# Hardware loops of two, five, eight and nine matmuls in an attention decode kernel, and a float32 turn of rows into columns per four heads

## The chip, the cores and the metric

The kernel runs on one core of a Trainium2 chip. The metric is the device time of one execution in microseconds (us), lower is better. Engines: PE multiplies matrices (PEld is its loading of weights, PEq or PEldq its sequencer), DVE is the vector engine, ACT the scalar engine, POOL the GpSimd engine; SP issues DMA transfers from a queue of its own. Each engine works through its own list of instructions in order and waits on semaphores that others raise.

## What is computed

A decode step for one token of width 640: a modulated layer norm, attention with 32 heads over a cache of 16384 positions of 128 each, and a gated feed-forward part. Cut to what matters:

```python
mod = (silu(c) @ w_mod).reshape(1, 6, 1, 640)        # c: (1, 640), w_mod: (640, 3840)
sa, ca, ga, sb, cb, gb = mod[:, 0], ..., mod[:, 5]
h = layernorm(x) * (1 + ca) + sa
q = (h @ wq).reshape(1, 1, 32, 128)                  # wq: (640, 4096)
scores = q . k_cache * 128 ** -0.5                   # k_cache, v_cache: (1, 32, 16384, 128)
o = softmax(scores) @ v_cache
x = x + ga * (o.reshape(1, 1, 4096) @ wo)            # wo: (4096, 640)
h = layernorm(x) * (1 + cb) + sb
x = x + gb * ((silu(h @ w_gate) * (h @ w_up)) @ w_down)   # F = 1728
```

All inputs are bfloat16. The caches are 268 of the 290 MB that are read.

## The kernel before

Every instruction is put down as an operation with an engine, a position in time (`pos`) and the operations that it depends on. `emit` sorts each engine's operations by position, and each engine then runs them in that order. There is no other scheduler: where an operation stands in its engine's queue is its position.

Sizes: H = 32 heads, TT = 128 positions per partition, KC = 5 pieces of 128 of the width, GQ = 4. `TK(h)` is the nominal start of head h, 20 + 19.8 h; `TL` is that of the last head.

**Start.** SP issues w_mod, wq, the four pieces of K of head 0 and K of head 1. PE multiplies the first two of w_mod's six parts (`mod_mm_a`), then q for all heads in eight groups (L352), each copied by ACT to `qbc`. Behind them in PE's queue stands `mod_mm_b` at position 4.5: the other four parts, 4 x 5 columns of five 128x1 matmuls each (100), from `f_mod` (L330), all written out. ACT copies its result (`mod_b`, L369, position 4.6). The operation `onep_b` on DVE (L370) reads that copy; it stands at `TK(0) + 19.3`, ahead of all DVE work of head 1.

**One head.** DVE multiplies K by q (L433), folds the products three times (L435, L442), sums (L445) and takes the largest (L448). POOL takes the largest over partitions (`gm`, L451), ACT scales it (`nb`, L453) and exponentiates (L455); POOL sums (`L`, L458), ACT forms the reciprocal (`lnl`, `rl`, L460 and L462). Then PE makes the value product (L471): 32 matmuls of four columns of P with 512 columns of V, so that the four 128-wide diagonal blocks of a 4x512 result hold the sum. Two matmuls stand ahead of a hardware loop, two behind it, and the loop has seven turns of `PVB` = 4 (L476). ACT scales the result into `acc_sb` (L483, four partitions, float32), and `diag` (L490) turns the rows into a column of `OT_ps` with four float32 matmuls against `ident_f`, one head at a time. ACT copies it (`on`, L511), spreads it over `Z` (L514), and once for a group of heads one matmul (L518) and one copy (`as`, L520) put the group in the order in which wo's rows lie. The groups are 8, 8, 8 and 4 heads; heads 28 to 31 (from `HD` on) go without a group, straight into `On` (L523).

**Queues.** SP's queue has, for each head, K of head h + 1 at `TK(h) + 8.8` (waits for the sum of head h - 1, whose place it takes) and V of head h just behind it at `TK(h) + 8.9` (waits for the value product of head h - 2). ACT's queue has `acc` of head h at `TK(h) + 28.6`, which is ahead of `nb` and `exp` of head h + 1 at `TK(h+1) + 19.2` and `+ 19.4`. PE's queue at the end: value product of head 30, its `diag`, then wo for the groups (`f_wo`, L559, positions from `TL + 29.45`, written out: 28 rows of five matmuls), wo for heads 28 to 30 (`TL + 29.48`), the last head (L501, `TL + 29.5`), wo for head 31 (`TL + 29.8`), layer norm, gate, up, down.

**The last head** has V in three pieces (`VSPLIT`: 64, 32 and 32 of the 128 positions), and 128 written-out matmuls of 128x128 by one column, straight into the column of `OT_ps`.

**The end.** The transfers of the feed-forward weights take the place of K and wait for the last head's sum. Gate and up (L623) have 70 matmuls each, down (L641) 70 in five pieces.

Of the kernel before, what the change touches and what calls it, by code (L numbers as in the profile page):

```python
# [7 lines left out]
F32 = mybir.dt.float32  # L8
ALU = mybir.AluOpType
ACTF = mybir.ActivationFunctionType  # L10
# [26 lines left out]
class _Plan:  # L37
# [104 lines left out]
def build(nc, A_x, A_k, A_v, A_wq, A_wo, B_wg, B_wu, B_wd, c_in, w_mod, out):  # L142
    H, S, Dh = A_k.shape[1], A_k.shape[2], A_k.shape[3]
    D = A_x.shape[2]
    F = B_wg.shape[1]
    assert Dh == 128 and D % 128 == 0 and S % 128 == 0
    KC = D // 128
    TT = S // 128
# [2 lines left out]
    FCH = NF + (1 if FR else 0)  # L151
    NP2 = NF // 2
    GQ = 4
    PVB = 4

    GROUPS = [(0, 8), (8, 8), (16, 8), (24, 4)]
    HD = 28
# [10 lines left out]
    with es:  # L168
# [3 lines left out]
        def sb(name, shape, dtype):  # L172
            return es.enter_context(nc.sbuf_tensor(name, list(shape), dtype))
# [17 lines left out]
        wg_v = kflat[:, 0:KC * F].rearrange("p (k n) -> p k n", k=KC)  # L191
        wu_v = kflat[:, KC * F:2 * KC * F].rearrange("p (k n) -> p k n", k=KC)
        wd_v = kflat[:, 2 * KC * F:2 * KC * F + FCH * D].rearrange("p (k n) -> p k n", k=FCH)
        acc_sb = sb("acc_sb", [4, 2, 512], F32)
        ident_f = sb("ident_f", [4, 4], F32)
        qbc = sb("qbc", [128, H, 128], BF16)
        S_sb = sb("S_sb", [128, 2, TT], F32)
        P_sb = sb("P_sb", [128, 2, TT], BF16)
# [19 lines left out]
        rl = sb("rl", [128, H], F32)  # L218
# [106 lines left out]
        def f_mod(e, wv, m0, m1, cols):  # L325
            last = None
            for m in range(m0, m1):
                for k in range(KC):
                    for kd in range(KC):
                        last = e.matmul(mod_ps[:, m * KC + k:m * KC + k + 1],  # L330
                                        lhsT=wv[:, kd, cols(m * D, k)], rhs=silu_c[:, kd:kd + 1],
                                        start=(kd == 0), stop=(kd == KC - 1))
            return last
# [31 lines left out]
        o_q_all = list(o_q.values())  # L365


        o_mod_b = op(PE, 4.5, lambda e: f_mod(e, wm_v, 2, 6, lambda o, k: slice(o + 128 * k, o + 128 * (k + 1))), deps=[d_wm, o_h], name="mod_mm_b")
        o_modc = op(ACT, 4.6, lambda e: e.activation(out=modb[:], in_=mod_ps[:, 2 * KC:6 * KC], func=ACTF.Copy), deps=[o_mod_b], name="mod_b")  # L369
        o_onep_b = op(DVE, TK(0) + 19.3, lambda e: e.tensor_scalar_add(out=onep_b[:], in0=modb[:, 2 * KC:3 * KC], scalar1=1.0), deps=[o_modc], name="onep_b")  # L370
        ga, sb_, gb = modb[:, 0:KC], modb[:, KC:2 * KC], modb[:, 3 * KC:4 * KC]
# [32 lines left out]
        load_k(0)  # L404
        load_k(1)

        o_idf = op(ACT, 4.7, lambda e: e.activation(out=ident_f[:], in_=ident[0:4, 0:4], func=ACTF.Copy), deps=[o_ident], name="ident_f")
        o_msk, o_e8 = {}, {}
        for n in msk:
            o_msk[n] = op(DVE, TK(0) + 19.0, lambda e, n=n: e.tensor_reduce(  # L410
# [8 lines left out]
        for h in range(H):  # L419
# [46 lines left out]
            if h < H - 1:  # L466


                def f_pv(e, s2=s2):
                    def one(t, at, start=False, stop=False):  # L470
                        return e.matmul(acc_ps[s2][0:4, :], lhsT=P_sb[:, s2, bass.ds(t, 4)],  # L471
                                        rhs=vbig[:, bass.ds(at, 512)], start=start, stop=stop)
                    v0 = s2 * TT * 128
                    one(0, v0, start=True)
                    one(4, v0 + 512)
                    with e.Fori(0, (TT - 16) // (4 * PVB)) as i:  # L476
                        for u in range(PVB):
                            one(i * (4 * PVB) + (8 + 4 * u), i * (512 * PVB) + (v0 + 1024 + 512 * u))
                    one(TT - 8, v0 + 128 * (TT - 8))
                    return one(TT - 4, v0 + 128 * (TT - 4), stop=True)  # L480
                o_pvlast[h] = op(PE, base + 28.0, f_pv, deps=[o_exp[h], d_v[h][0], o_acc[h - 2] if h >= 2 else o_qev[H // GQ - 1],
                                                              o_qev[H // GQ - 2]], name="pv%d" % h)
                o_acc[h] = op(ACT, base + 28.6, lambda e, h=h, s2=s2: e.activation(  # L483
                    out=acc_sb[:, s2], in_=acc_ps[s2][0:4, :], func=ACTF.Copy, scale=rl[0:4, h:h + 1]),
                    deps=[o_pvlast[h], o_rl, o_diag[h - 2] if h >= 2 else None], name="acc%d" % h)

                def f_diag(e, h=h, s2=s2):
                    last = None
                    for i in range(4):
                        last = e.matmul(OT_ps[:, h:h + 1], lhsT=acc_sb[:, s2, 128 * i:128 * (i + 1)], rhs=ident_f[:, i:i + 1],  # L490
                                        start=(i == 0), stop=(i == 3))
                    return last
                o_diag[h] = op(PE, base + 28.8, f_diag, deps=[o_acc[h], o_idf], name="diag%d" % h)
                done, sc = o_diag[h], 1.0
            else:

                for c in range(len(VSPLIT) - 1):
                    def f_pv(e, h=h, s2=s2, c=c):
                        last = None
                        for t in range(VSPLIT[c], VSPLIT[c + 1]):  # L500
                            last = e.matmul(OT_ps[:, h:h + 1], lhsT=vring[:, s2, t, :], rhs=P_sb[:, s2, t:t + 1],  # L501
                                            start=(t == 0), stop=(t == TT - 1))
                        return last
                    prev = op(PE, base + 29.5 + 0.05 * c, f_pv, deps=[o_exp[h], d_v[h][c], prev], name="pv%d_%d" % (h, c))
                o_pvlast[h] = prev
                done, sc = prev, rl[:, h:h + 1]
            if h < HD:
                g = [i for i, (h0, n) in enumerate(GROUPS) if h0 <= h < h0 + n][0]
                h0, n = GROUPS[g]
                jw = 128 // n  # L510
                o_on[h] = op(ACT, base + 29.0, lambda e, h=h, sc=sc: e.activation(  # L511
                    out=on_f[:, h:h + 1], in_=OT_ps[:, h:h + 1], func=ACTF.Copy, scale=sc),
                    deps=[done, o_rl], name="on%d" % h)
                o_z[h] = op(ACT, base + 29.2, lambda e, h=h, g=g, n=n, o=(h - h0) * jw, jw=jw: e.activation(  # L514
                    out=Z[:, g, o:o + jw], in_=msk[n][:], func=ACTF.Copy, scale=on_f[:, h:h + 1]),
                    deps=[o_on[h], o_msk[n]], name="z%d" % h)
                if h == h0 + n - 1:
                    o_am = op(PE, base + 29.4, lambda e, g=g, n=n: e.matmul(A_ps[:, 0:n], lhsT=Z[:, g], rhs=e8[n][:], start=True, stop=True),  # L518
                              deps=[o_z[i] for i in range(h0, h0 + n)] + [o_e8[n], o_as[g - 1] if g else None], name="am%d" % g)
                    o_as[g] = op(ACT, base + 29.6, lambda e, h0=h0, n=n: e.activation(out=A_sb[:, h0:h0 + n], in_=A_ps[:, 0:n], func=ACTF.Copy),  # L520
                                 deps=[o_am], name="as%d" % g)
            else:
                o_on[h] = op(ACT, base + 29.0 + (0.7 if h == H - 1 else 0.0), lambda e, h=h, sc=sc: e.activation(  # L523
                    out=On[:, h - HD:h - HD + 1], in_=OT_ps[:, h:h + 1], func=ACTF.Copy, scale=sc),
                    deps=[done, o_rl], name="on%d" % h)


        TO = TL + 9.0
# [2 lines left out]
        while a < len(GROUPS):  # L531
            b = a
            while b < len(GROUPS) and GROUPS[b][1] == GROUPS[a][1]:
# [6 lines left out]
            a = b  # L540
        d_wo1 = plan.dma(TO + 0.1, wo_v[:, HD:H, :], A_wo[HD * 128:H * 128, :].rearrange("(k p) n -> p k n", p=128),
                         "wo1", deps=[o_mod_b, o_mod], name="dma_wo_rows")
        wo_seq = [(k, g) for g, (h0, n) in enumerate(GROUPS) for k in range(h0, h0 + n)] + [(k, None) for k in range(HD, H)]
        o_wo = []
        for g in list(range(len(GROUPS))) + [None] * (H - HD):
            if g is not None:
                ks = [k for k, gg in wo_seq if gg == g]
                deps, pos = [o_as[g], d_wo[g]], TL + 29.45 + 0.005 * g
            else:
                k = HD + len(o_wo) - len(GROUPS)  # L550
                ks = [k]
                deps, pos = [o_on[k], d_wo1], TL + (29.48 + 0.001 * (k - HD) if k < H - 1 else 29.8)

            def f_wo(e, ks=ks):
                last = None
                for k in ks:
                    rhs = A_sb[:, k:k + 1] if k < HD else On[:, k - HD:k - HD + 1]
                    for cc in range(KC):
                        last = e.matmul(attn_ps[:, cc:cc + 1], lhsT=wo_v[:, k, 128 * cc:128 * (cc + 1)], rhs=rhs,  # L559
                                        start=(k == 0 and cc == 0), stop=(k == H - 1 and cc == KC - 1), skip_group_check=True)  # L560
                return last
            o_wo.append(op(PE, pos, f_wo, deps=deps, name="wo%d" % len(o_wo)))


        HX = H // 2
# [135 lines left out]
```

## Time and profile before

| | us |
|---|---|
| median of three runs | 686.17 (685.95 to 686.21) |
| the profiled execution | 685.94 |
| its span, first to last instruction | 684.2 |
| PE busy | 352.1 (51%) |
| DVE busy | 617.5 (90%) |
| ACT busy | 79.9 (12%) |
| POOL busy | 376.6 (55%) |

A row of a view's group or timeline has: when it starts, how long it takes (or the busy time of a group), the engine, the line of the kernel, the operation, what is written and what is read, the shape, the count, and in brackets the idle time just ahead and what ended it. The page's strips divide the span into 40 equal slices; a digit is the busy share of a slice in tenths. Matmuls are pipelined, so their durations overlap. Instructions that only PE's sequencer runs (register arithmetic, moves, branches) are not counted as busy; the view of a single source line lists them under PEldq, with the least, the median and the largest duration in ns.

Some groups that the change touches, before:

```profile
L490 PE MATMUL psb<-ident_f,acc_sb 4*128 4x1 f32 x248 | 32.5, 248 | 23.9 <-ACT acc_sb L483 23.9
L483 ACT ACTIVATE acc_sb<-psb,rl 4x512 f32<-4x512 f32 x31 | 21.0, 679 | 165.1 <-PE psb L471 165.1
L514 ACT ACTIVATE Z<-msk,on_f 128x16 bf16<-128x16 f32 (+1 forms) x28 | 8.7, 310 | 0.9
L511 ACT ACTIVATE on_f<-psb 128x1 f32<-128x1 f32 x28 | 4.8, 171 | 31.9 <-PE psb L490 30.7
```

### The profile page before, as it was taken

The numbers are of one execution on the slowest core, as the hardware profiler recorded it, in microseconds if no ns is written. First come the engines' busy times: TensorE is split into PE (matmuls) and PEld (weight loads), VectorE is DVE, ScalarE is ACT, GpSimd is POOL, SyncE is SP. The second block draws the span as 40 slices with busy tenths as digits, with TensorE's granted clock in tenths as the row PEclk, the third lists the DMA queues.
The fourth block names the chain that finished last, engine by engine and source line by source line (L and its number), as shares of the span: only waits on it lengthen the run. The fifth ranks groups of instructions, "written<-read, shape, count | busy, mean of one in ns | idle before, by whom it ended". The sixth has DMA issues, their size and how long they took to land.

```text
span 684.2 us, 6294 instructions
## 1 busy us (share of the span) xinstructions
PE 352.1 (51%) x1951; PEld 151.0 (22%) x1952; DVE 617.5 (90%) x226; ACT 79.9 (12%) x281; POOL 376.6 (55%) x71
## 2 busy tenths in 40 slices
PE   2335245565555444556544544656544446565554
PEld 1122022222212112222211212222121112221254
DVE  0299999999999999999999999999999999999911
ACT  1111011011101111011101111011011110110010
POOL 0004765655567765655567766655564656555600
PEclk9967666767777776776777776676677766766765
DMA  9999999999999999999999999999999999999996
GB/s 374 418 437 431 431 436 433 430 431 433 435 428 429 429 433 429 435 431 430 437 433 432 432 427 431 428 433 429 432 433 433 435 435 428 431 431 432 412 413 267
DMA packets 13689, 290.70 MB, mean 425 GB/s; under 512 B 1318, under 2 KB 2024, under 8 KB 4200
## 3 DMA queue, kind: packets, MB, share of 16 engines
q1 hardware_dynamic: 13668, 290.48, 99.2%
q8 instruction: 10, 0.16, 0.1%
q14 instruction: 7, 0.06, 0.0%
q10 hardware_dynamic: 4, 0.00, 0.0%
HBM read 290.48 MB, written 0.00 MB: 425 GB/s over the span
## 4 chain that ended last, share of the span: by engine, by line
DVE 79%; DMA 18%; SPq 2%; issue 1%; PE 0%; ACT 0%; DVEq 0%
DVE kring L433 35%; DVE kring L435 18%; DVE kring L442 14%; DMA kring<-in_A_k_cache_dram 12%; DVE S_sb L445 9%; DMA vbig<-in_A_wq_dram 4%; DMA kring<-in_B_w_down_dram 2%; SPq L71 2%; DVE pm L448 1%; PE psb L352 0%; PE psb L641 0%; ACT qbc L356 0%; DVE e L415 0%; DVE msk L410 0%; PE psb L649 0%
## 5 line engine op out<-in xcount | busy, mean ns | idle before, releaser
L471 PE MATMUL psb<-vbig,P_sb 128*4 128x512 bf16 (+1 forms) x992 | 285.4, 458 | 267.0 <-ACT P_sb L455 200.3
L451 POOL PARTITION_ALL_REDUCE gm<-pm x32 | 254.8, 7963 | 226.7 <-DVE pm L448 220.6
L433 DVE TENSOR_TENSOR kring<-kring,qbc 128x16384 bf16<-128x16384 bf16 (+1 forms) x35 | 278.4, 7954 | 14.0 <-ACT qbc L356 12.9
L471 PEld LDWEIGHTS psb<-vbig,P_sb 128*4 128x4 bf16 (+1 forms) x992 | 94.6, 97 | 444.7 <-ACT P_sb L455 243.5
L435 DVE TENSOR_TENSOR kring<-kring 128x8192 bf16<-128x8192 bf16 (+1 forms) x35 | 142.1, 4059 | 1.2
L458 POOL PARTITION_ALL_REDUCE Ls<-rs x32 | 120.8, 3774 | 29.9 <-ACT P_sb L455 29.9
L442 DVE TENSOR_TENSOR kring<-kring 128x4096 bf16<-128x4096 bf16 x64 | 112.5, 1758 | 2.2
L445 DVE TENSOR_REDUCE S_sb<-kring 128x128 f32<-128x2048 bf16 x32 | 73.2, 2286 | 1.1
L490 PE MATMUL psb<-ident_f,acc_sb 4*128 4x1 f32 x248 | 32.5, 248 | 23.9 <-ACT acc_sb L483 23.9
L483 ACT ACTIVATE acc_sb<-psb,rl 4x512 f32<-4x512 f32 x31 | 21.0, 679 | 165.1 <-PE psb L471 165.1
L490 PEld LDWEIGHTS psb<-ident_f,acc_sb 4*128 4x128 f32 x248 | 29.8, 186 | 39.6 <-ACT acc_sb L483 39.6
L453 ACT ACTIVATE nb<-gm 128x1 f32<-128x1 f32 x32 | 6.5, 202 | 213.2 <-POOL gm L451 213.2
L460 ACT ACTIVATE lnl<-Ls 128x1 f32<-128x1 f32 x32 | 6.5, 203 | 124.7 <-POOL Ls L458 124.7
L352 PE MATMUL psb<-vbig,h_col 128*128 128x512 bf16 x39 | 9.9, 421 | 10.6 <-DMA vbig<-in_A_wq_dram 10.6
L598 DVE TENSOR_TENSOR tt<-attn_bf,modb 128x5 f32<-128x5 bf16 x1 | 0.2, 166 | 15.3 <-ACT attn_bf L597 15.3
L455 ACT ACTIVATE P_sb<-S_sb,nb 128x128 bf16<-128x128 f32 x32 | 12.9, 402 | 1.2
L448 DVE TENSOR_REDUCE pm<-S_sb 128x1 f32<-128x128 f32 x32 | 9.2, 286 | 1.1
L514 ACT ACTIVATE Z<-msk,on_f 128x16 bf16<-128x16 f32 (+1 forms) x28 | 8.7, 310 | 0.9
L511 ACT ACTIVATE on_f<-psb 128x1 f32<-128x1 f32 x28 | 4.8, 171 | 31.9 <-PE psb L490 30.7
L352 PEld LDWEIGHTS psb<-vbig,h_col 128*128 128x128 bf16 x40 | 4.2, 108 | 15.9 <-DMA vbig<-in_A_wq_dram 10.3
L356 ACT ACTIVATE qbc<-psb 128x512 bf16<-128x512 f32 x8 | 4.8, 598 | 23.2 <-PE psb L352 23.2
L330 PE MATMUL psb<-silu_c,wreg 128*128 128x1 bf16 x150 | 4.8, 168 | 5.0 <-DMA wreg<-in_w_mod_dram 5.0
(74 smaller groups left out, 67.0 us busy)
## 6 DMA issues: line engine op xcount, KB each, us to landing
kring<-in_A_k_cache_dram SPq DMA_DIRECT2D x31, 4096.0 KB, 18.3
vbig<-in_A_v_cache_dram SPq DMA_DIRECT2D x31, 4096.0 KB, 27.5
vbig<-in_A_wq_dram SPq DMA_DIRECT2D x1, 5120.0 KB, 26.3
wreg<-in_w_mod_dram SPq DMA_DIRECT2D x1, 4800.0 KB, 14.4
kring<-in_A_k_cache_dram SPq DMA_DIRECT2D x4, 1024.0 KB, 31.3
wreg<-in_A_wo_dram SPq DMA_DIRECT2D x1, 3840.0 KB, 37.9
kring<-in_B_w_gate_dram SPq DMA_DIRECT2D x1, 2160.0 KB, 18.4
kring<-in_B_w_up_dram SPq DMA_DIRECT2D x1, 2160.0 KB, 23.8
```

Source lines behind the costliest of these rows:

```text
L71: return e.dma_start(out_ap, in_ap)
L352: last = e.matmul(q_ps[b][:, 0:n * 128], lhsT=h_col[:, k:k + 1].broadcast_to([128, 128]), rhs=wv[:, k, n0:n0 + n * 128], start=(k == 0), s ...
L433: o_m = op(DVE, base + 3.3 * c, lambda e, ksl=ksl, qb=qb: e.tensor_tensor(out=ksl, in0=ksl, in1=qb, op=ALU.mult), deps=[d_k[h][c], o_qbc[h ...
L435: fd.append(op(DVE, base + 3.3 * c + 2.2 + (6.6 if npc == 1 else 0.0), lambda e, ksl=ksl: e.tensor_tensor(out=ksl[:, :, 0:64], in0=ksl[:, ...
L442: prev = [op(DVE, base + 15.5 + 1.5 * i, lambda e, kslot=kslot, w=w: e.tensor_tensor(out=kslot[:, :, 0:w], in0=kslot[:, :, 0:w], in1=kslot ...
L445: o_red[h] = op(DVE, base + 18.2, lambda e, s2=s2, kslot=kslot, w=w: e.tensor_reduce(out=S_sb[:, s2], in_=kslot[:, :, 0:w], axis=AX.X, op= ...
L448: o_max = op(DVE, base + 18.5, lambda e, h=h, s2=s2: e.tensor_reduce(out=pm[:, h:h + 1], in_=S_sb[:, s2], axis=AX.X, op=ALU.max), deps=[o_ ...
L451: o_gm = op(POOL, base + 19.0, lambda e, h=h: e.partition_all_reduce(gm[:, h:h + 1], pm[:, h:h + 1], channels=128, reduce_op=bass.bass_isa ...
L458: o_L = op(POOL, base + 20.0, lambda e, h=h: e.partition_all_reduce(Ls[:, h:h + 1], rs[:, h:h + 1], channels=128, reduce_op=bass.bass_isa. ...
L471: return e.matmul(acc_ps[s2][0:4, :], lhsT=P_sb[:, s2, bass.ds(t, 4)], rhs=vbig[:, bass.ds(at, 512)], start=start, stop=stop)
L483: o_acc[h] = op(ACT, base + 28.6, lambda e, h=h, s2=s2: e.activation(out=acc_sb[:, s2], in_=acc_ps[s2][0:4, :], func=ACTF.Copy, scale=rl[0 ...
L490: last = e.matmul(OT_ps[:, h:h + 1], lhsT=acc_sb[:, s2, 128 * i:128 * (i + 1)], rhs=ident_f[:, i:i + 1], start=(i == 0), stop=(i == 3))
```

## The change

Five edits, four of them on PE.

1. **Value loop.** `PVB` is 2 instead of 4. One matmul stands ahead of the loop and one behind it, and the loop has 15 turns of two.
2. **Rows into columns per four heads.** `acc_sb` has 128 partitions. Head j of four writes partitions 32 j to 32 j + 3 in one of two halves. One `diag` for four heads (for three at the end) sums over all 128 partitions against `sel`, which picks one of the four rows for each head; `acc_sb` is set to zero once on DVE (`acc_zero`, position 2.3). The copies `on` take four columns at once; `Z` is still filled head by head.
3. **Second half of w_mod.** 19 turns of a loop of five matmuls, and the last column written out.
4. **wo for the groups.** One operation instead of four: five matmuls written out, then 27 turns of five. It waits for all four groups and all their transfers.
5. **The last head.** 63 of the first piece's 64 matmuls in seven turns of nine, the second piece's 32 in four turns of eight; the third piece stays written out.

```diff
-    PVB = 4
+    PVB = 2
...
-        acc_sb = sb("acc_sb", [4, 2, 512], F32)
-        ident_f = sb("ident_f", [4, 4], F32)
+        acc_sb = sb("acc_sb", [128, 2, 512], F32)
+        sel = sb("sel", [128, 4, 4], F32)
...
-        o_mod_b = op(PE, 4.5, lambda e: f_mod(e, wm_v, 2, 6, lambda o, k: slice(o + 128 * k, o + 128 * (k + 1))), deps=[d_wm, o_h], name="mod_mm_b")
+        def f_mod_b(e):
+            def column(i):
+                last = None
+                for kd in range(KC):
+                    last = e.matmul(mod_ps[:, bass.ds(i + 2 * KC, 1)], lhsT=wreg[:, bass.ds(i * 128 + (kd * 6 + 2) * D, 128)],
+                                    rhs=silu_c[:, kd:kd + 1], start=(kd == 0), stop=(kd == KC - 1))
+                return last
+            with e.Fori(0, 4 * KC - 1) as i:
+                column(i)
+            return column(4 * KC - 1)
+        o_mod_b = op(PE, 4.5, f_mod_b, deps=[d_wm, o_h], name="mod_mm_b")
...
+        o_az = op(DVE, 2.3, lambda e: e.memset(acc_sb[:], 0.0), deps=[o_cc, o_xc0, o_sc], name="acc_zero")
...
                     one(0, v0, start=True)
-                    one(4, v0 + 512)
-                    with e.Fori(0, (TT - 16) // (4 * PVB)) as i:
+                    with e.Fori(0, (TT - 8) // (4 * PVB)) as i:
                         for u in range(PVB):
-                            one(i * (4 * PVB) + (8 + 4 * u), i * (512 * PVB) + (v0 + 1024 + 512 * u))
-                    one(TT - 8, v0 + 128 * (TT - 8))
+                            one(i * (4 * PVB) + (4 + 4 * u), i * (512 * PVB) + (v0 + 512 + 512 * u))
                     return one(TT - 4, v0 + 128 * (TT - 4), stop=True)
...
+                if j == GQ - 1 or h == H - 2:
+                    def f_diag(e, h0=h - j, n=j + 1, gb_=gb_):
+                        last = None
+                        for i in range(4):
+                            last = e.matmul(OT_ps[:, h0:h0 + n], lhsT=acc_sb[:, gb_, 128 * i:128 * (i + 1)], rhs=sel[:, i, 0:n],
+                                            start=(i == 0), stop=(i == 3))
+                        return last
+                    o_diag[h] = op(PE, base + 28.8, f_diag, deps=o_acc[h - j:h + 1] + [o_sel], name="diag%d" % h)
...
                     def f_pv(e, h=h, s2=s2, c=c):
+                        def one(t):
+                            return e.matmul(OT_ps[:, h:h + 1], lhsT=vbig[:, bass.ds(t * 128 + s2 * TT * 128, 128)], rhs=P_sb[:, s2, bass.ds(t, 1)],
+                                            start=(isinstance(t, int) and t == 0), stop=(isinstance(t, int) and t == TT - 1))
+                        ta, tb = VSPLIT[c], VSPLIT[c + 1]
                         last = None
-                        for t in range(VSPLIT[c], VSPLIT[c + 1]):
-                            last = e.matmul(OT_ps[:, h:h + 1], lhsT=vring[:, s2, t, :], rhs=P_sb[:, s2, t:t + 1],
-                                            start=(t == 0), stop=(t == TT - 1))
+                        if c < len(VSPLIT) - 2:
+                            if c == 0:
+                                one(0)
+                                ta = 1
+                            n = max(n for n in range(1, 11) if (tb - ta) % n == 0)
+                            with e.Fori(0, (tb - ta) // n) as i:
+                                for u in range(n):
+                                    one(i * n + (ta + u))
+                            return None
+                        for t in range(ta, tb):
+                            last = one(t)
                         return last
...
+        def f_wo_cols(e):
+            for cc in range(KC):
+                e.matmul(attn_ps[:, cc:cc + 1], lhsT=wo_v[:, 0, 128 * cc:128 * (cc + 1)], rhs=A_sb[:, 0:1],
+                         start=(cc == 0), stop=False, skip_group_check=True)
+            with e.Fori(0, HD - 1) as i:
+                for cc in range(KC):
+                    e.matmul(attn_ps[:, cc:cc + 1], lhsT=wreg[:, bass.ds(i * D + (D + 128 * cc), 128)], rhs=A_sb[:, bass.ds(i + 1, 1)],
+                             start=False, stop=False, skip_group_check=True)
+            return None
+        o_wo.append(op(PE, TL + 29.45, f_wo_cols, deps=o_as + d_wo, name="wo_cols"))
```

`bass.ds(a, n)` is a slice of n elements from a, where a may be formed from the loop's counter; `e.Fori(0, n)` is a loop that the engine's own sequencer runs.

More of the change, by code (lines that the diff above doesn't have):

```diff
@@ L405, in build @@
         load_k(1)
-        o_idf = op(ACT, 4.7, lambda e: e.activation(out=ident_f[:], in_=ident[0:4, 0:4], func=ACTF.Copy), deps=[o_ident], name="ident_f")
+        o_sel = op(ACT, 4.7, lambda e: e.activation(
+            out=sel[:], in_=ident[:].rearrange("p (j c) -> p c j", j=4)[:, 0:4, :], func=ACTF.Copy), deps=[o_ident], name="sel")
+        o_az = op(DVE, 2.3, lambda e: e.memset(acc_sb[:], 0.0), deps=[o_cc, o_xc0, o_sc], name="acc_zero")
         o_msk, o_e8 = {}, {}
@@ L480, in f_pv @@
                     return one(TT - 4, v0 + 128 * (TT - 4), stop=True)
+                j, gb_ = h % GQ, (h // GQ) % 2
                 o_pvlast[h] = op(PE, base + 28.0, f_pv, deps=[o_exp[h], d_v[h][0], o_acc[h - 2] if h >= 2 else o_qev[H // GQ - 1],
                                                               o_qev[H // GQ - 2]], name="pv%d" % h)
-                o_acc[h] = op(ACT, base + 28.6, lambda e, h=h, s2=s2: e.activation(
-                    out=acc_sb[:, s2], in_=acc_ps[s2][0:4, :], func=ACTF.Copy, scale=rl[0:4, h:h + 1]),
-                    deps=[o_pvlast[h], o_rl, o_diag[h - 2] if h >= 2 else None], name="acc%d" % h)
@@ L487, in f_diag @@
[L487 to L494, printed above, removed]
+                o_acc[h] = op(ACT, base + 28.6, lambda e, h=h, s2=s2, j=j, gb_=gb_: e.activation(
+                    out=acc_sb[32 * j:32 * j + 4, gb_], in_=acc_ps[s2][0:4, :], func=ACTF.Copy, scale=rl[0:4, h:h + 1]),
+                    deps=[o_pvlast[h], o_rl, o_diag[h - 2 * GQ + GQ - 1 - j] if h >= 2 * GQ else o_az], name="acc%d" % h)
@@ L498, in f_pv @@
                     def f_pv(e, h=h, s2=s2, c=c):
+                        def one(t):
+                            return e.matmul(OT_ps[:, h:h + 1], lhsT=vbig[:, bass.ds(t * 128 + s2 * TT * 128, 128)], rhs=P_sb[:, s2, bass.ds(t, 1)],
+                                            start=(isinstance(t, int) and t == 0), stop=(isinstance(t, int) and t == TT - 1))
+                        ta, tb = VSPLIT[c], VSPLIT[c + 1]
                         last = None
-                        for t in range(VSPLIT[c], VSPLIT[c + 1]):
-                            last = e.matmul(OT_ps[:, h:h + 1], lhsT=vring[:, s2, t, :], rhs=P_sb[:, s2, t:t + 1],
-                                            start=(t == 0), stop=(t == TT - 1))
+                        if c < len(VSPLIT) - 2:
[9 more added lines that the diff above has]
+                            last = one(t)
                         return last
-                    prev = op(PE, base + 29.5 + 0.05 * c, f_pv, deps=[o_exp[h], d_v[h][c], prev], name="pv%d_%d" % (h, c))
+                    prev = op(PE, base + 29.5 + 0.05 * c, f_pv, deps=[o_exp[h], d_v[h][c]], name="pv%d_%d" % (h, c))
                 o_pvlast[h] = prev
-                done, sc = prev, rl[:, h:h + 1]
             if h < HD:
@@ L510, in build @@
                 jw = 128 // n
[L511 to L516, printed above, removed]
+                if j < GQ - 1:
+                    continue
+                o_on[h] = op(ACT, base + 29.0, lambda e, h=h: e.activation(
+                    out=on_f[:, h - GQ + 1:h + 1], in_=OT_ps[:, h - GQ + 1:h + 1], func=ACTF.Copy),
+                    deps=[o_diag[h]], name="on%d" % h)
+                for hh in range(h - GQ + 1, h + 1):
+                    o_z[hh] = op(ACT, base + 29.2, lambda e, h=hh, g=g, n=n, o=(hh - h0) * jw, jw=jw: e.activation(
+                        out=Z[:, g, o:o + jw], in_=msk[n][:], func=ACTF.Copy, scale=on_f[:, h:h + 1]),
+                        deps=[o_on[h], o_msk[n]], name="z%d" % hh)
                 if h == h0 + n - 1:
@@ L521, in build @@
                                  deps=[o_am], name="as%d" % g)
[L522 to L525, printed above, removed]
+            elif h == H - 2:
+                o_on[h] = op(ACT, base + 29.0, lambda e: e.activation(
+                    out=On[:, 0:H - 1 - HD], in_=OT_ps[:, HD:H - 1], func=ACTF.Copy), deps=[o_diag[h]], name="on%d" % h)
+                for hh in range(HD, h):
+                    o_on[hh] = o_on[h]
+            elif h == H - 1:
+                o_on[h] = op(ACT, base + 29.7, lambda e, h=h: e.activation(
+                    out=On[:, h - HD:h - HD + 1], in_=OT_ps[:, h:h + 1], func=ACTF.Copy, scale=rl[:, h:h + 1]),
+                    deps=[prev, o_rl], name="on%d" % h)
         TO = TL + 9.0
@@ L542, in build, with f_wo @@
                          "wo1", deps=[o_mod_b, o_mod], name="dma_wo_rows")
-        wo_seq = [(k, g) for g, (h0, n) in enumerate(GROUPS) for k in range(h0, h0 + n)] + [(k, None) for k in range(HD, H)]
         o_wo = []
[L545 to L554, printed above, removed]
-                last = None
[L556 to L560, printed above, removed]
+        def f_wo_cols(e):
[8 more added lines that the diff above has]
+        o_wo.append(op(PE, TL + 29.45, f_wo_cols, deps=o_as + d_wo, name="wo_cols"))
+        for k in range(HD, H):
+            def f_wo(e, k=k):
+                last = None
+                for cc in range(KC):
+                    last = e.matmul(attn_ps[:, cc:cc + 1], lhsT=wo_v[:, k, 128 * cc:128 * (cc + 1)], rhs=On[:, k - HD:k - HD + 1],
+                                    start=False, stop=(k == H - 1 and cc == KC - 1), skip_group_check=True)
                 return last
-            o_wo.append(op(PE, pos, f_wo, deps=deps, name="wo%d" % len(o_wo)))
+            o_wo.append(op(PE, TL + (29.48 + 0.001 * (k - HD) if k < H - 1 else 29.8), f_wo, deps=[o_on[k], d_wo1], name="wo%d" % k))
         HX = H // 2
```

## The prediction

> **What bounds the kernel now.** I read the page's strips first, then the timeline at both ends, then the instructions of the loop that already exists.
>
> ```profile
> span 684.2 us, 6294 instructions
> DMA  9999999999999999999999999999999999999996
> q8 instruction: 10, 0.16, 0.1%
> ```
>
> The transfers run full from the first slice to the last but one. The chain of waits gives DVE 79% of the span, and both are true. From 51.70 us on, DVE starts a head every 19.28 us, and the transfers deliver a head's K and V in 19.42 us (K landings 48.1, 67.5, 86.96). Until 492 us DVE is never idle between heads, and from 495 us it waits for K. Thirty periods from 51.70 end at 630.2 us, while the last head's first product starts at 632.06. So DVE has 1.9 us to spare in the whole run, and the transfers have none. The hand-over from PE to DVE in the first head is this:
>
> ```profile
> 37.82 2.64 PE L330 MATMUL psb<-silu_c,wreg 128*128 128x1 bf16 x100
> 40.50 0.19 ACT L369 ACTIVATE modb<-psb 128x20 f32<-128x20 f32 x1 [1.88 <-PE psb L330]
> 51.63 0.16 DVE L370 TENSOR_SCALAR onep_b<-modb 128x5 f32<-128x5 f32 x1
> 51.70 8.68 DVE L433 TENSOR_TENSOR kring<-kring,qbc 128x16384 bf16<-128x16384 bf16 x1
> ```
>
> The second half of the modulation product takes 2.64 us and is ready 11 us before DVE reads it, in the instruction just ahead of the second head. The end of the run on PE:
>
> ```profile
> 651.33 1.05 PE L490 MATMUL psb<-ident_f,acc_sb 4*128 4x1 f32 x8 [0.77 <-ACT acc_sb L483]
> 652.31 3.68 PE L559 MATMUL psb<-A_sb,wreg 128*128 128x1 bf16 x140
> 659.42 1.85 PE L501 MATMUL psb<-P_sb,vbig 128*128 128x1 bf16 x64 [1.69 <-DMA vbig<-in_A_v_cache_dram]
> 664.30 0.67 PE L501 MATMUL psb<-P_sb,vbig 128*128 128x1 bf16 x19 [1.47 <-DMA vbig<-in_A_v_cache_dram]
> 670.05 2.25 PE L623 MATMUL psb<-h_col,kring 128*128 128x1 bf16 x70 [1.04 <-DVE h_col L607]
> 675.37 2.25 PE L623 MATMUL psb<-h_col,kring 128*128 128x1 bf16 x70 [3.06 <-DMA kring<-in_B_w_up_dram]
> 679.48 0.69 PE L641 MATMUL psb<-gu_col,kring 128*128 128x1 bf16 x20 [0.57 <-DMA kring<-in_B_w_down_dram]
> ```
>
> PE works off wo and the last head between transfers and waits again for w_up and w_down. It is near the end without setting it. Written out, a 128x1 product costs it 26 ns (3.68 us / 140) to 29 ns (1.85 / 64).
>
> **What a loop costs on PE.** The view of one line's instructions also lists what PE's sequencer runs, for the value loop (L471, loop line L476):
>
> ```profile
> L471 PEldq FUSED_REGOPS  x868: 51/74/79, 58.2 to 649.3; - x174
> L476 PEldq FUSED_REGOPS  x217: 78/78/82, 58.1 to 648.7; - x109
> L476 PEldq ALU_OP  x217: 36/36/42, 58.8 to 649.4; - x109
> L476 PEldq COMPARE_BRANCH  x217: 76/213/353, 58.9 to 649.5; - x109
> ```
>
> That is 31 heads of 7 turns: per turn one register instruction for the counter, one for each of the four matmuls, a count and a branch. What the register instructions do is in the program of the kernel before: additions and multiplications that form addresses, at most six to an instruction. Their starts in the trace (medians of 217 turns) are 0, 137, 266, 424, 576, 729 and 845 ns, and the next turn begins 271 ns after the branch, together 1116 ns. So a turn costs 137 ns ahead and 116 + 271 = 387 ns behind, 129 ns for the first matmul (three address steps, 51 ns, were left over for it) and 153 ns for each further one (six steps, three for each of two addresses, 74 ns; the rest is the gap and the issue of load and matmul). The turn is about as long while PE's granted clock is 0.5 as at 1.0 (1116 and 1096 ns in the last such loop, from 641.9 us), so this is sequencer time. It is hidden now, because four 512-column matmuls fill the array for 4 x 216 = 864 to 4 x 427 = 1708 ns. A 128x1 matmul fills it for 26 ns, so there the sequencer will set the pace.
>
> **Part by part.**
>
> *w_mod, second half.* 100 written-out matmuls become 19 turns of five and one last column. The output column is the same for five matmuls. If its address is kept, each matmul needs three new steps, about 130 ns as the first one above: 137 + 129 + 4 x 130 + 387 = 1173 ns, 19 turns 22.3 us. If it is worked out each time, six steps: 1269 ns, 24.1 us. I take the kept one: the counter's multiples are formed once for a turn in the existing loop, since four register instructions suffice for eight addresses. PE issues it from about 37.0 us (its last q product goes out then), ends at 59.5, the copy on ACT at 59.75, onep_b at 60.1. The second head's product starts at 60.1 instead of 51.70, **8.4 us later** (10.2 by the other price). Behind onep_b in DVE's queue is every later head. Behind the copy in ACT's queue are nb and exp of head 0, so head 0's value product starts at about 60.5 instead of 57.96. K3 is issued at 79.2 instead of 70.8; V1 landed at 77.25, so the transfers run dry for some 3 us. K31 then lands about 635 us, before DVE asks for it at 630.2 + 8.4 = 638.6. DVE, not DMA, carries the delay to the end.
>
> *Value loop.* A turn of two matmuls is 137 + 129 + 158 + 387 = 811 ns, 15 turns 12.2 us, with the first and last matmul 12.7 us, against 8.69 us for head 30. Hidden in heads 0 to 29: ACT needs the result 18.3 us after the product's start (the next nb), PE has 19.28 us per head. V's issue, which waits for the product two heads back, comes some 3 us after the K ahead of it in SP's queue, whose transfer takes 9.7 us; without that cover each head would lose those 3 us. The next K's issue waits for DVE longer than that. Only in head 30 is it on the path: 4.0 us.
>
> *Rows into columns.* 31 groups of eight passes of 1.05 us become eight, 28 on_f copies become seven. That takes some 24 us from PE and 4 us from ACT, both off the path; the last one stays where it was, behind acc30 (0.68 us), 1.74 us from the end of value product 30 to wo. The zeroing of acc_sb (eight times the 128x128 memset of 0.165 us, 1.3 us) falls into DVE's idle 12.88 us ahead of 30.69. Ahead of nb31 and exp31, ACT now waits for value product 30; they come at about 664 us, needed only at 695.
>
> *wo.* 140 matmuls in 3.68 us become five and 27 turns of five, 27 x 1.173 = 31.7 us (34.3 by six steps). It now waits for all groups and the wo transfers (landed by 652.60, 654.38 for the rows behind it), long done.
>
> *Last head.* 63 products in seven turns of nine and 32 in four turns of eight. Here V's address is formed from the sum of counter and offset, then multiplied by 128, then moved by the ring slot, doubled and based: five steps, and three for P, eight together. At six to an instruction that is two: 74 + 59 (gap) and about 46 + 79, 258 ns per matmul. Turns of 137 + 9 x 258 + 387 = 2846 and 137 + 8 x 258 + 387 = 2588 ns: 19.9 + 10.4 = 30.3 us. If the multiplication is taken apart beforehand, six steps: 1885 x 7 + 1731 x 4 = 20.1 us. I take 30.3, as the existing loop doubles after adding and takes nothing apart. Before, both pieces took 2.87 us.
>
> **Sum**, from the profiled execution. Head 30's value product starts at 641.87 - 632.06 = 9.81 us behind the last head's first DVE product: 638.6 + 9.8 = 648.4. It ends at 661.1; wo starts at 662.85; five columns and 27 turns to 694.7; three written-out rows (0.45) to 695.2; the looped pieces to 725.5; the last 32 (0.93 us at 29 ns) to 726.4. From there to the end was 684.2 - 665.9 = 18.3 us; the waits for w_up and w_down go, since both have landed (up then follows gate at once, ends 8.7 us behind the value product, down 2.3 us, the rest 2.6): 13.9 us. Span 740.3; outside the span lie 685.94 - 684.2 = 1.7 us. **742 us**, +8.1% on the median of 686.17, which is 0.03% over the profiled execution.
>
> [...]
>
> **Rivals.**
> 1. *The last head's addresses cost six steps.* 742 - 10.2 = 732 us. For it: nothing in the rows speaks of multiplication behind an addition. Chance 0.27.
> 2. *The shared address is worked out for each matmul.* 1.8 us more in w_mod and 2.6 in wo: 746 us. For it: each matmul of the present loop has its own register instruction. Chance 0.16.
> 3. *The w_mod loop hides behind head 0.* It must end by 51.3 us, 14.3 us for 95 matmuls, 150 ns each with branch: 742 - 8.4 = 734. Against it: 279 ns each today (1116/4). Chance 0.04.
> 4. *Loops that lie across a code block fetch at each turn.* Two of 31 value loops took 8.79 instead of 7.72 us, with a code packet (queue q8) in them: 1.07 us per fetch, and if each of wo's 27 turns paid it, 771 us. Against it: both paid once in seven turns. Chance 0.04. [...]
> 5. *Not slower: the loops fit into PE's waits at the end.* From 652.3 us PE has 12.0 us until the last V piece lands and 3.06 us ahead of w_up, 15 us for 230 looped products. That decides at about 60 ns each with branch. Then w_down's landing at 680.85 sets the end again: 686 us, at best 0.5 us less (all code fetches are 0.22 MB at 425 GB/s). Against it: the present loop is four times as slow per matmul. Chance 0.03.
>
> **Chances and range.** Forecast 0.45, the rivals as above, 0.01 for none of them. The range, 728 to 752, takes in rivals 1, 2 and 3 and some 4 us for what the turn's length may differ; outside it lie rivals 4 and 5 and the tails of the others, somewhat under 2 in 10. A change under 0.2% could not be told from none here. Faster 0.01, within 0.2% 0.03 (rival 5), slower 0.96.
>
> **What will show it.** Right if the modulation copy comes near 59 us and DVE idles some 8 us ahead of the second head; if wo's looped products take over 30 us with about 1.2 us a turn; if looped products of the last head have 150 to 260 ns each, and up follows gate without a wait for w_up. Value products should take 12 to 13 us with no idle DVE between heads. Wrong if PE's sequencer gets through a turn of five in well under 1 us, or if DVE's heads lengthen.

## The result, and the profile after

| | before | after |
|---|---|---|
| median, us | 686.17 (685.95 to 686.30, five runs) | 739.13 (738.94 to 739.46, five runs) |
| ratio | | 1.0776 (95% interval 1.0764 to 1.0787) |
| span of the profiled execution, us | 684.2 | 737.2 |

The change makes the kernel 53 us slower; 742 us was forecast, 728 to 752 as the range. The page of the changed kernel, its strips and its code packets:

```profile
span 737.2 us, 7294 instructions
DMA  9999799999999999999999999999999999999100
q8 instruction: 5, 0.08, 0.0%
```

Two slices carry the story. The transfers dip early, in the fifth slice (74 to 92 us), and they end with the 38th: over the last 50 us next to nothing is moved (1 GB/s) and PE's chain sets the time. Fewer code packets are fetched (five on queue q8 instead of ten), which buys nothing that shows.

The timeline of the changed kernel at the first hand-over, DVE and ACT:

```profile
59.37 0.19 ACT L379 ACTIVATE modb<-psb 128x20 f32<-128x20 f32 x1 [19.95 <-PE psb L372]
59.59 0.17 DVE L380 TENSOR_SCALAR onep_b<-modb 128x5 f32<-128x5 f32 x1 [7.41 <-ACT modb L379]
59.67 8.68 DVE L445 TENSOR_TENSOR kring<-kring,qbc 128x16384 bf16<-128x16384 bf16 x1
```

The copy of the modulation comes at 59.37 instead of 40.50 us. DVE sits 7.41 us ahead of `onep_b`, an instruction of 0.17 us, and the second head starts at 59.67 instead of 51.70.

What that does to the transfers, from the windows of both kernels (sum of time; then the busy time of PE, PEld, DVE, ACT, POOL; the granted clock; the share of the transfers; GB/s). Before:

```profile
65.00:85.00 20.00, 7.12 (x28) 2.78 (x26) 19.83 (x7) 2.26 (x8) 12.35 (x2) 0.67 1.01 434
```

After:

```profile
65.00:85.00 20.00, 6.36 (x22) 1.74 (x20) 19.83 (x7) 1.08 (x3) 9.48 (x2) 0.76 0.78 319
```

K of head 3 is issued at 78.74 instead of 70.77 us, V of head 1 has landed at 76.89, and 0.23 of 20 us, 4.6 us, are lost.

The end of the run on PE, timeline of the changed kernel:

```profile
663.69 0.68 PE L581 MATMUL psb<-A_sb,wreg 128*128 x5 [0.48 <-issue]
...
690.93 0.70 PE L581 MATMUL psb<-A_sb,wreg 128*128 x5 [0.43 <-issue]
...
692.21 2.42 PE L510 MATMUL psb<-P_sb,vbig 128*128 128x1 bf16 x10
695.09 2.28 PE L510 MATMUL psb<-P_sb,vbig 128*128 x9 [0.46 <-issue]
697.82 2.28 PE L510 MATMUL psb<-P_sb,vbig 128*128 x9 [0.46 <-issue]
...
716.62 0.44 PE L510 MATMUL psb<-P_sb,vbig 128*128 x2 [0.51 <-issue]
717.34 1.50 PE L510 MATMUL psb<-P_sb,vbig 128*128 x6 [0.29 <-issue]
719.30 0.43 PE L510 MATMUL psb<-P_sb,vbig 128*128 x2 [0.46 <-issue]
...
726.64 4.42 PE L653 MATMUL psb<-h_col,kring 128*128 128x1 bf16 x140 [1.04 <-DVE h_col L637]
731.40 3.17 PE L671 MATMUL psb<-gu_col,kring 128*128 128x1 bf16 x70 [0.34 <-DVE gu_col L662]
```

Each turn of a loop stands as a row of its own, with idle time ahead of it that nothing but PE's own issue ends ("<-issue"). Five products of wo come every 1.135 us (663.69 to 690.93 in 24 turns), nine of the last head every 2.73. Only in the last head's second piece is a turn of eight broken into two rows (716.62 and 717.34); rival 4 below comes back to it. Gate and up are one row of 140 now: all weights had landed by 686.43 us, and no wait for a transfer is left. What the sequencer did in these two loops, from the views of their lines:

```profile
L581 PEldq FUSED_REGOPS  x135: 42/46/46, 661.3 to 691.3; - x135
L579 PEldq COMPARE_BRANCH  x27: 76/208/208, 662.0 to 691.6; - x27
L510 PEldq FUSED_REGOPS  x179: 42/60/79, 692.3 to 721.2; - x179
```

wo has one register instruction for each product, the last head nearly two (179 for 95).

### The profile page after: what moved, and what is told of

Read it like the earlier page. It is cut to its first block, busy times and chain, and to the rows that moved or that the text cites. A ratio compares the mean times of both kernels' runs of the same rounds, so it can differ in the third digit from the quotient of the medians.

```text
span 737.2 us, 7294 instructions
## 1 busy us (share of the span) xinstructions
PE 412.2 (56%) x1768; PEld 143.3 (19%) x1768; DVE 617.8 (84%) x227; ACT 73.7 (10%) x258; POOL 381.0 (52%) x71
## 4 chain that ended last, share of the span: by engine, by line
DVE 78%; PE 11%; issue 5%; DMA 4%; POOL 1%; ACT 0%; SPq 0%; DVEq 0%
DVE kring L445 35%; DVE kring L447 18%; DVE kring L454 14%; DVE S_sb L457 9%; DMA vbig<-in_A_wq_dram 4%; PE psb L510 3%; PE psb L581 2%; PE psb L372 2%; PE psb L483 1%; PE psb L352 1%; POOL gm L463 1%; DVE pm L460 1%; PE psb L653 1%; PE psb L671 0%; PE psb L501 0%
## 5 line engine op out<-in xcount | busy, mean ns | idle before, releaser
L483 PE MATMUL psb<-vbig,P_sb 128*4 128x512 bf16 (+1 forms) x992 | 329.4, 456 | 252.8 <-ACT P_sb L467 198.4
L463 POOL PARTITION_ALL_REDUCE gm<-pm x32 | 262.2, 8195 | 221.7 <-DVE pm L460 221.7
L483 PEld LDWEIGHTS psb<-vbig,P_sb 128*4 128x4 bf16 (+1 forms) x992 | 84.4, 85 | 495.7 <-issue 255.1
L510 PE MATMUL psb<-P_sb,vbig 128*128 (+1 forms) x128 | 18.6, 179 | 11.7 <-issue 5.6
L581 PE MATMUL psb<-A_sb,wreg 128*128 x135 | 18.1, 182 | 11.5 <-issue 11.5
L372 PE MATMUL psb<-silu_c,wreg 128*128 128x1 bf16 x100 | 13.0, 180 | 7.8 <-issue 7.7
L581 PEld LDWEIGHTS psb<-A_sb,wreg 128*128 x135 | 13.7, 103 | 15.9 <-issue 13.6
L510 PEld LDWEIGHTS psb<-P_sb,vbig 128*128 (+1 forms) x128 | 10.9, 104 | 19.3 <-issue 10.7
L501 PE MATMUL psb<-sel,acc_sb 128*128 128x4 f32 (+1 forms) x64 | 8.6, 258 | 6.1 <-ACT acc_sb L494 6.1
L372 PEld LDWEIGHTS psb<-silu_c,wreg 128*128 (+1 forms) x100 | 9.7, 102 | 11.2 <-issue 9.0
```

Of the source, the lines that this page charges most:

```text
L372: last = e.matmul(mod_ps[:, bass.ds(i + 2 * KC, 1)], lhsT=wreg[:, bass.ds(i * 128 + (kd * 6 + 2) * D, 128)], rhs=silu_c[:, kd:kd + 1], sta ...
L463: o_gm = op(POOL, base + 19.0, lambda e, h=h: e.partition_all_reduce(gm[:, h:h + 1], pm[:, h:h + 1], channels=128, reduce_op=bass.bass_isa ...
L510: return e.matmul(OT_ps[:, h:h + 1], lhsT=vbig[:, bass.ds(t * 128 + s2 * TT * 128, 128)], rhs=P_sb[:, s2, bass.ds(t, 1)], start=(isinstanc ...
L581: e.matmul(attn_ps[:, cc:cc + 1], lhsT=wreg[:, bass.ds(i * D + (D + 128 * cc), 128)], rhs=A_sb[:, bass.ds(i + 1, 1)], start=False, stop=Fa ...
```

## The experiments

All times are medians, beside 685.9 to 686.2 us for the kernel before on the same chip. "Less" is less than the changed kernel's 739.13 us. The first four kernels undo one edit of the changed kernel each.

**The last head written out** (edit 5 undone).

```diff
-                        if c < len(VSPLIT) - 2:
+                        if False:
```

> The changed kernel with the last head's 95 looped products written out again, all else kept. Theory (PE's sequencer sets the pace of the loops at the end, nothing hides it): the looped pieces took 29.3 us (692.2 to 721.5), written out they take 95 x 29 ns = 2.8 us, so 739.1 - 26.5 = 712.6 us. Rival (the end is held by something else, so that the loops overlap it): less than half of that, above 726 us.

Measured 712.73 us (ratio to before 1.0394, interval 1.0377 to 1.0411), 26.4 us less than the changed kernel. The whole head is one row of its timeline, 3.55 us for 128 products:

```profile
692.72 3.55 PE L510 MATMUL psb<-P_sb,vbig 128*128 128x1 bf16 x128
```

All of the loop's time was on the path.

**wo written out** (edit 4 undone).

```diff
-            with e.Fori(0, HD - 1) as i:
+            for i in range(HD - 1):
```

> The changed kernel with wo's 27 turns written out, all else kept. Theory: 30.6 us of loop (27 x 1.135) become 135 x 26 ns = 3.5 us, 739.1 - 27.1 = 712.0 us. Rival (PE's lower granted clock at the end makes the matmuls slow, not the loop): the written-out rows run at the same slow pace and the time stays above 726 us.

Measured 712.15 us (1.0381, 1.0363 to 1.0398), 27.0 us less. The timeline speaks against the rival that the clock makes the matmuls slow: the same products at 26.5 ns each, at the same place in the run.

```profile
662.60 3.58 PE L581 MATMUL psb<-A_sb,wreg 128*128 128x1 bf16 x135
```

**The second half of w_mod written out** (edit 3 undone).

```diff
-            with e.Fori(0, 4 * KC - 1) as i:
+            for i in range(4 * KC - 1):
```

> The changed kernel with the second half of w_mod written out. Theory: DVE's second head starts at 51.7 again instead of 59.67 us, but the last head's K then lands at 632.0 us, after DVE could start it (630.2), so of 8.0 us only 638.17 - 632.06 = 6.1 us come back: 733.0 us. Rival A (the delay is carried in full): 731.1 us. Rival B (only the loops at the end cost anything): 739.1 us.

Measured 732.42 us (1.0679, 1.0662 to 1.0697), 6.7 us less: nearer to the forecast of 6.1 than to 8.0, and clearly not zero. About 0.7 us of it is not w_mod's: the looped second piece of the last head takes 9.34 us here and 10.05 in the changed kernel (see rival 4 below). DVE's second head starts at 51.81 us.

**The value loop in turns of four** (edit 1 undone).

```diff
-    PVB = 2
+    PVB = 4
...
+                    one(4, v0 + 512)
+                    with e.Fori(0, (TT - 16) // (4 * PVB)) as i:
...
+                    one(TT - 8, v0 + 128 * (TT - 8))
```

> The changed kernel with the value loop as before (seven turns of four). Theory: only head 30's product is on the path, 12.27 us against 8.69 us (9.85 in some heads): 735.5 to 736.7 us. Rival (31 products are each 3.6 us longer and delay V, so that more comes back): under 733 us; rival (hidden everywhere): 739.1 us.

Measured 736.14 us (1.0739, 1.0721 to 1.0757; its runs 734.9 to 737.6), 3.0 us less. Head 30's product took 9.37 us in its profile, against 12.27. That is one product's saving, not 31. The runs spread over 2.7 us, and the profiled one is the fastest of them, with 0.7 us less in the last head's second piece too, so how the 3.0 us divide is not settled.

The next three ask what a loop's time is made of.

**Fewer address steps in the last head.** Data, matmuls and turns stay.

```diff
-                            return e.matmul(OT_ps[:, h:h + 1], lhsT=vbig[:, bass.ds(t * 128 + s2 * TT * 128, 128)],
+                            return e.matmul(OT_ps[:, h:h + 1], lhsT=vbig[:, bass.ds(at, 128)],
...
-                                    one(i * n + (ta + u))
+                                    one(i * n + (ta + u), i * (n * 128) + ((ta + u) * 128 + s2 * TT * 128))
```

> The changed kernel with the last head's V address formed as a multiple of the counter plus a constant, so that each looped product needs six address steps (one register instruction) instead of eight (two); matmuls, turns and data are the same. Theory (address steps set the pace): 153 instead of 253 ns for each of 95 products, 9.5 us less: 729.6 us. Rival (a looped matmul has its price whatever the address): 739.1 us.

Measured 729.27 us (1.0625, 1.0607 to 1.0643), 9.9 us less. One register instruction for each product is left (95 instead of 179), and a turn of nine takes 1.87 us (696.14 to 698.01) instead of 2.73:

```profile
696.14 1.43 PE L511 MATMUL psb<-P_sb,vbig 128*128 x9 [0.44 <-issue]
698.01 1.42 PE L511 MATMUL psb<-P_sb,vbig 128*128 x9 [0.44 <-issue]
```

```profile
L511 PEldq FUSED_REGOPS  x95: 46/74/79, 692.3 to 711.9; - x95
```

The way in which an index is written cost 10 us here.

**wo in turns of fifteen.**

```diff
-            with e.Fori(0, HD - 1) as i:
-                for cc in range(KC):
-                    e.matmul(..., lhsT=wreg[:, bass.ds(i * D + (D + 128 * cc), 128)], rhs=A_sb[:, bass.ds(i + 1, 1)], ...)
+            with e.Fori(0, (HD - 1) // 3) as i:
+                for r in range(3):
+                    for cc in range(KC):
+                        e.matmul(..., lhsT=wreg[:, bass.ds(i * (3 * D) + ((r + 1) * D + 128 * cc), 128)],
+                                 rhs=A_sb[:, bass.ds(i * 3 + (r + 1), 1)], ...)
```

> The changed kernel with wo in nine turns of fifteen matmuls instead of 27 of five. Theory: a turn costs 512 ns beside its matmuls (1135 - 5 x 124.5), a matmul 124.5, two of fifteen 28 more for the other operand's address: turn 2.44 us, nine 21.9 instead of 30.6 us, 730.4 us. Rival A (all cost is per matmul): 739.1 us. Rival B (beside the matmuls a turn costs some 200 ns only): 18 x 0.2 - 0.5 = 3.1 us less, 736 us.

Measured 730.00 us (1.0639, 1.0621 to 1.0657), 9.1 us less, by theory 8.7. All rows of wo together take 21.49 us in the profile, against 29.80 in the changed kernel: 8.3 us of the 9.1 are theirs. A turn of fifteen takes 2.485 us (676.20 to 678.68 and on). Eighteen turns fewer saved 0.5 us each, so the price of a turn as such is shown, apart from that of its matmuls. In the changed kernel the branch alone takes 208 ns (the L579 row), and the next turn's first instruction starts 266 ns after the branch starts.

**Each looped matmul of wo twice.**

```diff
                 for cc in range(KC):
+                    for _ in range(2):
                         e.matmul(attn_ps[:, cc:cc + 1], lhsT=wreg[:, bass.ds(i * D + (D + 128 * cc), 128)], ...)
```

> The changed kernel with each looped matmul of wo issued twice with the same addresses; 27 of wo's 32 rows count twice in the output. Theory (register instructions set the pace, matmuls are nearly free): 135 more at 20 to 29 ns, 2.7 to 3.9 us: 742 to 743 us. Rival (a matmul in a loop costs its 125 ns as such): 135 x 0.125 = 16.9 us more, 756 us.

Measured 738.68 us (1.0763, 1.0745 to 1.0781), no more than the changed kernel: 135 additional matmuls cost nothing that shows, less than I expected; wo's rows take 29.84 us against 29.80. Ten in a turn, and the turns still come every 1.13 us (664.64 to 665.78):

```profile
664.64 0.73 PE L582 MATMUL psb<-A_sb,wreg 128*128 x10 [0.41 <-issue]
665.78 0.73 PE L582 MATMUL psb<-A_sb,wreg 128*128 x10 [0.41 <-issue]
```

The last four ask where a loop is on the path at all.

**The reader of w_mod one head later.** The loop stays; `onep_b` is not needed before the end.

```diff
-        o_onep_b = op(DVE, TK(0) + 19.3, ...
+        o_onep_b = op(DVE, TK(1) + 19.3, ...
```

> The changed kernel with the loop of w_mod kept, and onep_b, its reader on DVE, one head later in DVE's queue. Theory (the loop costs time only through the place of its reader in DVE's queue): as with w_mod written out, 733.0 us. Rival (the later exponential of head 0, or the loop as such, holds the heads): 736 to 739 us.

Measured 733.38 us (1.0687, 1.0669 to 1.0705), 5.8 us less, though the loop is as long as it was. DVE's second head starts at 52.00 us, and `onep_b` finds its input ready:

```profile
71.29 0.16 DVE L380 TENSOR_SCALAR onep_b<-modb 128x5 f32<-128x5 f32 x1
71.36 8.69 DVE L445 TENSOR_TENSOR kring<-kring,qbc 128x16384 bf16<-128x16384 bf16 x1
```

So the loop cost time through its reader's place in DVE's queue. Of the 1.0 us to the kernel with w_mod written out, the traces place 0.7 in the last head, whose looped second piece takes 10.05 us here against 9.34 there. The other 0.3 come ahead of wo: head 30's product waits for its V until 642.28 us, against 641.98.

**Edits 1 and 2 alone** (w_mod, wo and the last head written out).

> The first two edits alone: the value loop of 15 turns and one diag per four heads; w_mod, wo and the last head written out as before. Theory (both are off the path while transfers set the end; head 30's longer product uses up PE's wait ahead of the last V piece): as before, 686.2 us, within 0.2%. Rival (the 3.6 us of the value loop stay on the path as in the changed kernel): 689.8 us.

Measured 685.92 us, as before (1.0002, interval 0.9993 to 1.0011). The value loop of 15 turns and the turn of rows into columns per four heads cost nothing while the transfers set the end. They gain nothing either: the time that they take off or put onto PE is waiting time (PE sits 6.98 us ahead of head 30's product until its V lands, and 3.02 ahead of w_up). Edit 2 was not undone alone; it is in all eleven kernels of this section.

**Edits 2 and 4 alone** (wo's loop; value loop of four, w_mod and last head written out).

> Edits 2 and 4 alone: diag per four heads and wo's loop; value loop of four, w_mod and last head written out. Theory (wo's loop first uses up the 12 us that PE waits for the last V piece and the waits for w_up and w_down, and only the rest lengthens the run): wo from 652.3 us, loop 30.8 us, three rows 0.5, 128 products at 29 ns 3.7, 14.7 us from there to the end as in the changed kernel, 1.7 outside the span: 703.7 us. Rival (the loop costs what it gave back in the changed kernel, 27.0 us): 713.2 us.

Measured 704.13 us (1.0267, 1.0253 to 1.0281), 18.2 us over before. The loop that gave back 27.0 us in the changed kernel costs 18.2 by itself, since PE's waits cover most of the rest: in the kernel before, 3.7 us of its idle time ended with V (L501), 3.1 with w_up (L623) and 0.6 with w_down (L641), and here none of these waits is left (gate and up are one row of 140).

**Edits 2 and 3 alone** (w_mod's loop; value loop of four, wo and last head written out).

> Edits 2 and 3 alone: diag per four heads and the loop of w_mod; value loop of four, wo and last head written out. Theory (the loop makes DVE late, DVE's late K issue lets the transfers run dry, and the transfers set the end): in the changed kernel the last piece of w_down lands at 686.43 instead of 680.85 us, so 5.6 us more, 691.5 us. Rival A (the dry time is only the 3 us that the prediction worked out): 689.2 us. Rival B (PE's long end was what made the delay visible, without it it is hidden): 686.0 us.

Measured 692.12 us (1.0085, 1.0072 to 1.0099), 6.1 us over before. The end is a matter of transfers again; its PE timeline waits for w_up and w_down:

```profile
682.19 2.25 PE L655 MATMUL psb<-h_col,kring 128*128 128x1 bf16 x70 [2.94 <-DMA kring<-in_B_w_up_dram]
686.32 0.69 PE L673 MATMUL psb<-gu_col,kring 128*128 128x1 bf16 x20 [0.58 <-DMA kring<-in_B_w_down_dram]
```

Transfers that ran dry once near 78 us (share 0.73 between 65 and 85 us in this kernel) never catch up.

No version beats the kernel before; edits 1 and 2 alone equal it.

## Why the prediction was right

Its chain of times beside the trace of the changed kernel, in us:

| step | predicted | measured |
|---|---|---|
| second head starts on DVE | 60.1 | 59.67 |
| last head starts on DVE | 638.6 | 638.17 |
| value product of head 30 | 648.4 to 661.1 | 647.88 to 660.15 |
| wo starts | 662.85 | 661.83 |
| wo's loop ends | 694.7 | 691.6 |
| looped pieces of the last head | 695.2 to 725.5 | 692.2 to 721.5 |
| last head ends | 726.4 | 722.5 |
| span | 740.3 | 737.2 |

*The sequencer as the bound.* Shown by three kernels: fewer register instructions for the same matmuls took 9.9 us off, fewer turns 9.1, and twice the matmuls added nothing. Rival 5, that the loops fit into PE's waits, falls with the wo loop alone: 18.2 us over before.

*w_mod.* The turn of five was put at 1173 ns, and takes 1135: three address steps of the kind used here last 46 ns, not 51, and the count and the branch 363 ns, not 387. Rival 2, the shared address worked out for every matmul (1269 ns), is out. Rival 3, that the loop hides behind head 0, is out by DVE's 7.41 us.

*The dry transfers* were put at 3 us and lost 4.6. K of the last head landed at 637.82, not 635, only 0.35 us ahead of DVE. In the changed kernel that made no difference, and the statement that DVE and not DMA carries the delay holds, but barely: the margin was put at 3.6 us (638.6 - 635), and that 0.35 sufficed is luck. With PE's end taken away, the dry time is most of what w_mod's loop costs (6.1 us), and the 3 us would have been too little.

*The value loop.* 12.27 us for head 30, forecast 12.7; hidden in the other heads, as worked out (685.92 us with edits 1 and 2 alone). The 24 us of PE time that the new turn of rows into columns saves came to nothing.

*The last head.* 29.3 us, forecast 30.3. Eight address steps do make two register instructions (179 for 95 products), so rival 1 (732 us) is out; with six steps, the turn of nine takes 1.87 us, 1885 ns by the working.

*What the sum missed by 2.9 us* is 2.0 us in wo's loop (27 x 38 ns, and the first turn's register instructions run from 661.15 us, while PE still works on the rows ahead until 661.96), 0.4 us each in DVE's start and the value product, and 0.9 us in the last head with the rows ahead of it. Against it, the stretch from the last head to the end took 14.7 instead of 13.9 us: down takes 3.17 us for 70 matmuls where I had put 2.3, because a wait instruction of 51 ns stands between each two of its five pieces: at these four places 0.31 us pass from one weight load to the next, elsewhere 0.027.

*The parts don't add up, and need not.* Undoing one edit gives back 26.4, 27.0, 6.7 and 3.0 us, 63.1 in all, of a loss of 53.0. PE's waits for transfers cover the first part of a delay at the end, whichever loop uses them up: wo's loop gave back 27.0 us and costs 18.2 by itself, which is 8.8 of the 10.1 us. Some of the rest is the last head's looped second piece, 0.4 to 0.7 us shorter in three of these four kernels.

*Rival 4*, a fetch of 1.07 us at every turn, is out: wo's turns are even (1.12 to 1.16 us), and the trace has no code packet on queue q8 between 529.2 and 714.0 us. Its price came from two value loops of the kernel before; three more there had a packet in them and lost only some 0.3 us. But the packet at 714.0 us falls into the loop of the last head's second piece, and a turn of eight takes 2.68 us there (716.62 to 719.30). In the kernel with w_mod written out, which has no packet in this loop, it takes 2.46:

```profile
707.97 1.98 PE L510 MATMUL psb<-P_sb,vbig 128*128 x8 [0.46 <-issue]
710.43 2.00 PE L510 MATMUL psb<-P_sb,vbig 128*128 x8 [0.48 <-issue]
```

Seven kernels have this loop with the same addresses. The three without a packet in it need 9.34 to 9.36 us for the piece, the four with one 9.61 to 10.05. No experiment was made on this, so the cause stays open.

Code fetches account for little of what wo's loop costs: its rows, with no packet of q8 in the loop, take 29.80 us, against 3.70 written out.

## What to carry to other kernels

The price of a hardware loop was PE's sequencer time here: wo's turn of five took 1.135 us, and five written-out products take 0.13 (26.5 ns each). So count the register instructions and the branch of a turn in the trace, and loop only where the work of a turn takes longer than that, or where nothing waits for it. Two 512-column matmuls to a turn were too little here: head 30's product took 12.27 us, against 9.37 with four. Where a loop can't be avoided, make turns long (9.1 us less with fifteen products of wo to a turn), share addresses between matmuls (124 ns from one product's register instruction to the next in wo, 153 in the value loop before, which forms two addresses for each), and write an index as a multiple of the counter plus a constant (9.9 us less in the last head). And look who reads the result in another engine's queue: a reader that isn't needed for 600 us held every head behind it, and moving it back by one head gave 5.8 us.

## What the runs showed of the hardware

I had expected an additional matmul in a loop to cost 20 to 29 ns, near the 26.5 ns that a product of wo takes written out. Ten matmuls a turn took as long as five: the turns came every 1.13 us with either. In the changed kernel a register instruction of wo's loop takes 46 ns, and the next one starts 124 ns after it did. That a second load and matmul pair passes in what is left of this is an estimate from these two numbers. How many more would pass was not tried.
